# A fused attention and MLP block on one core: the second lower half of a step moved and written in place, and the keys' requests gathered

## The chip, the cores and the metric

The kernel runs on one core of a Trainium2 chip. The metric is device time in microseconds (us) of one launch; three runs of the kernel before gave 1380.38, 1377.33 and 1381.35 us, so a median of 1380.38 us. Traces come from a separate, profiled execution.

## The reference

For `x` of 1 x 2048 x 640 the kernel computes a parallel block: `xn` is the layer norm of `x`, and the output is `x` plus attention of `xn` plus an MLP of the layer norm of `xn`.

```
q, k, v = split(xn @ wqkv)                  # 32 heads of 20
p = softmax(q k^T * 20**-0.5)               # 2048 x 2048 for each head
A = (p v) @ wo
B = gelu(layernorm(xn) @ w1 + b1) @ w2 + b2 # 640 -> 1536 -> 640
out = x + A + B
```

All inputs are float32, and the kernel keeps nearly that precision on a 16-bit path: most operands are carried as a pair of 16-bit halves, an upper and a lower one, and a product is three matmuls of halves.

## The kernel before, in words

**Three stretches.** First (up to about 225 us) layer norm, the projections to queries, keys and values, and the splitting of weights into halves. Queries and keys go to DRAM scratch (`qkscr`), values stay on chip (`vfull`). Then the attention loop (about 225 to 1319 us), with the MLP's matmuls and the first part of the output projection poured between the attention's. Then the rest of the output projection.

**The attention loop.** Heads are taken four at a time (a quad). `VISITS` lists ten visits: quads 0 to 5 with four chunks of 512 queries each, then quads 6 and 7 twice with two chunks each: 32 rounds of one quad and one chunk (number 0 to 31 below). A round goes over 16 key blocks of 128 keys, two blocks to a step, so 256 steps. For each block `scores` (L766) makes two pairs of score tiles (L772, TensorE, into a PSUM pool of three) and ScalarE writes their exponentials to a float32 tile `pt` of 128 x 4 x 512 (L774).

**Split blocks.** In nine blocks of sixteen (`SPLIT`: 0, 2, 4, 6, 8, 9, 10, 12, 14) the probabilities are multiplied in halves. The upper half is no copy: `upper(pt)` (L776) reads the upper 16 bits of each float32 as bfloat16. The lower half is made by VectorE in `rest` (L780 to L786): `low = pt - upper(pt)`, written as float16 to a tile of its own from a rotation of two (L785). `pv` (L788) then multiplies with the values (L800): sixteen matmuls of 128 x 512 for the upper halves of two split blocks, four for each lower half, eight for a block that is not split. Block 9 is the only odd block that is split, so one step in eight has two lower halves; its step is the fifth of a round.

**Order around the change.** The instructions are recorded by hand in a fixed order (`manual_schedule`), and each engine works off its own list in that order. For an even block the list is: the block's scores and exponentials, `tick()`, `rest` of the previous step's odd block if that is split (block 9 alone), then `other()`, a measured portion of MLP or projection matmuls. For an odd block: scores and exponentials, `tick()`, `rest` of the even block of this step, then `pv` of the previous step. `tick()` advances every generator in the list `sides` by one piece. These pieces are VectorE's other work (the gelu chain L922 to L937, sums of the MLP's results L953, splitting of `wo` L739 to L744, the softmax division L883 to L911) and DMA requests on SyncE's queue, which issues them one after another. So VectorE's list around block 9 reads: lower half of block 8, the pieces of the tick of block 10, lower half of block 9, the pieces of the tick of block 11, lower half of block 10. TensorE's list there reads: scores of block 10, MLP matmuls, scores of block 11, `pv` of blocks 8 and 9, scores of block 12.

**Keys.** A visit needs its keys as two tiles of 61 rows twice (three copies of 20 rows, and a bias row, for each of two row groups). `load_keys` (L168) requests one half as six transfers from `qkscr` (L176) and two bias rows (L180), spread over five ticks, the bias rows last. The first half for the next visit is asked for at block 8 of a visit's last round, the second half at the first step of the visit, in `sides` behind the queries of the next round (`load_queries`, L148), which come one transfer a tick. Block 8 of that first round is the first to read the second half.

Of the kernel before, what the change touches and what calls it, by code (L numbers as in the profile page):

```python
# [10 lines left out]
F16 = mybir.dt.float16  # L11
# [7 lines left out]
P = 128  # L19
S, D, H, DH, F = 2048, 640, 32, 20, 1536  # L20
# [6 lines left out]
SPLIT = (1, 0) * 4 + (1, 1) + (1, 0) * 3  # L27
# [6 lines left out]
GRP = 2  # L34
# [14 lines left out]
def mha_mlp_kernel(tc, x, wqkv, wo, w1, b1, w2, b2, out):  # L49
    nc = tc.nc  # L50
# [3 lines left out]
    with (  # L54
# [17 lines left out]
        bscr = dram.tile([H + 1, S], F16, name="bscr")  # L72
# [75 lines left out]
        def load_queries(v, cc):  # L148

            q = VISITS[v][0]  # L150
            qs = stp.tile([P, 2, 512], F16, tag="qs", name="qs")
            qss[v, cc] = qs
            cols = slice(cc * 512, (cc + 1) * 512)
            for a in range(2):
                for i in range(3):
                    nc.sync.dma_start(qs[64 * a + i * DH : 64 * a + (i + 1) * DH], rows_of(qkscr[(0, 0, 1)[i]], 0, q, a, cols))
                    yield
            for a in range(2):
                h = 4 * q + a
                nc.sync.dma_start(qs[64 * a + 60 : 64 * a + 61], bscr[h : h + 3 : 2, cols].rearrange("(o p) t -> o p t", o=1))  # L160
                yield

        def rows_of(scr, r0, q, a, cols):

            r = r0 + 4 * q * DH
            return (scr[r : r + 4 * DH, cols].rearrange("(p a d) t -> a d p t", p=2, a=2)[a])

        def load_keys(v, half):  # L168

            q = VISITS[v][0]  # L170
            ks = stp.tile([P, 2, S // 2], F16, tag="ks", name="ks")
            kss[v, half] = ks
            cols = slice(half * 1024, (half + 1) * 1024)
            for a in range(2):
                for i in range(3):
                    nc.sync.dma_start(ks[64 * a + i * DH : 64 * a + (i + 1) * DH], rows_of(qkscr[(0, 1, 0)[i]], D, q, a, cols))  # L176
                    if i != 1:
                        yield
            for a in range(2):
                nc.sync.dma_start(ks[64 * a + 60 : 64 * a + 61], bscr[H : H + 1, None, cols].to_broadcast([1, 2, S // 2]))  # L180
            yield

        def load_first():
            parts = load_queries(0, 0), load_keys(0, 0)
            for _ in range(8):
                for p in parts:
                    next(p, None)
                yield
            yield from load_keys(0, 1)
# [8 lines left out]
        with tc.tile_pool(name="pa", bufs=2) as pa, tc.tile_pool(name="pa1", bufs=1) as pa1, tc.manual_schedule():  # L198
# [378 lines left out]
            pt = [pts[0][:, 0], pts[0][:, 1], pts[1][:, 0], pts[1][:, 1]]  # L577
# [114 lines left out]
        with ExitStack() as scope:  # L692
# [3 lines left out]
            ptp = pool(name="pt", bufs=2 * GRP)  # L696
# [4 lines left out]
            sides, patient = [], []  # L701
# [11 lines left out]
            def tick():  # L713
                t, taken[0] = taken[0], 0.0
                for its in (sides, patient):
                    for it in list(its):
                        if its is patient and t > 0 and it not in free:
                            continue
                        free.discard(it)
                        r = next(it, self_end)  # L720
                        if r is self_end:
                            its.remove(it)
                        elif r == WAIT:
                            free.add(it)
                        else:
                            t += r or 0.0
# [39 lines left out]
            def scores(v, cc, kb, pair, pt):  # L766

                qs, ks = qss[v, cc], kss[v, kb // 8]
                ps = psS.tile([P, 2, 512], F32, tag="s", name="s")
                for a in range(2):  # L770
                    rows = slice(64 * a, 64 * a + 61)
                    nc.tensor.matmul(ps[:, a, :], ks[rows, pair, kb % 8 * P : (kb % 8 + 1) * P], qs[rows, pair, :],  # L772
                                     start=True, stop=True)
                nc.scalar.activation(pt[:, 2 * pair : 2 * pair + 2], ps, AF.Exp, scale=QS)  # L774

            def upper(pt):  # L776

                return pt.bitcast(BF16).rearrange("p a (n t) -> p a n t", t=2)[:, :, :, 1]

            def rest(unit):  # L780

                kb, pt = unit[2:]
                if SPLIT[kb]:
                    low = ptp.tile([P, 4, 512], F16, tag="low", name="low", bufs=2)
                    nc.vector.tensor_sub(low, pt, upper(pt))  # L785
                    unit.append(low)  # L786

# [338 lines left out]
            def chain():  # L1126
                yield from mlp()
                yield from projection()


            with tc.manual_schedule():
                fill = chain()
                credit = 0.0 - next(fill)
                rate = 1.265
                groups = [(v, cc, kb) for v, (_, ccs) in enumerate(VISITS) for cc in ccs for kb in range(0, NKB, GRP)]
                prev = None

                runs = []

                def other():  # L1140

                    nonlocal credit
                    if not runs:
                        unit = next(fill)
                        if unit is None:
                            credit = 0.0
                            return
                        n, cost = unit
                        k = max(round((cost - credit) / rate) + 1, math.ceil(cost / CHUNK))
                        runs.extend(n * (i + 1) // k - n * i // k for i in range(k))  # L1150
                    for _ in range(runs.pop(0)):
                        credit -= next(fill)

                for v, cc, kb0 in groups:
                    units = []
                    for kb in range(kb0, kb0 + GRP):
                        pt = ptp.tile([P, 4, 512], F32, tag="p", name="p")
                        units.append([v, cc, kb, pt])
                        for pair in range(2):
                            scores(v, cc, kb, pair, pt)  # L1160
                        reading[0] = kb % GRP > 0 and prev is not None and prev[-1][2] == NKB - 1
                        tick()
                        if kb % GRP == 0:
                            if prev and SPLIT[prev[1][2]]:
                                rest(prev[1])
                            credit += rate
                            other()
                        else:
                            if SPLIT[kb - 1]:
                                rest(units[0])  # L1170
                            if prev:
                                pv(prev)
                            else:

                                credit += rate
                                other()
                    prev = units
                    ccs = VISITS[v][1]
                    if kb0 == 0:
                        if cc != ccs[-1]:  # L1180
                            sides.append(load_queries(v, cc + 1))
                        elif v + 1 < len(VISITS):
                            sides.append(load_queries(v + 1, VISITS[v + 1][1][0]))
                        if v and cc == ccs[0]:
                            sides.append(load_keys(v, 1))
                    if kb0 == NKB // 2 and cc == ccs[-1] and v + 1 < len(VISITS):
                        sides.append(load_keys(v + 1, 0))
                if SPLIT[prev[1][2]]:
                    rest(prev[1])
                n = 0  # L1190
                reading[0] = False
                ended[0] = True

                def more(k):
                    nonlocal n
                    for _ in range(k):
                        n += 1
                        cost = next(fill, 0)
                        if isinstance(cost, tuple):
                            cost = next(fill)  # L1200
                        tick()
                        if cost == 0:
                            return False
                    return True

                more(2)
                pv(prev)
                while more(1):
                    pass
                while sides or patient:  # L1210
                    tick()
                flag = nc.values_load(badi, min_val=0, max_val=1)
# [91 lines left out]
```

## Time and profile before

| what | value |
|---|---|
| median of three runs | 1380.38 us |
| the profiled execution's own time | 1382.86 us |
| its span, first to last instruction | 1380.9 us |
| around the span | 2.0 us |
| ScalarE busy | 1121.6 us, 81% |
| VectorE busy | 1102.9 us, 80% |
| TensorE granted clock, mean of the span | 0.991 |

The time outside the span is start and end of the launch. A busy time is the sum over an engine's instructions; for TensorE, whose matmuls overlap, it is near the span whenever the array is fed at all. "Idle before" in a row is the time that the engine stood still ahead of that instruction, with the instruction that released it. In a timeline the columns are start, duration, engine, line, operation, output and input, count, and in brackets the idle time.

### The profile page before, as it was taken

The page shows a single profiled execution, that of the slowest core. Times are in us where ns is not written, and L with a number is a line of the kernel's source. Part 1 is how long each engine was busy: PE and PEld are TensorE (multiplying, and loading weights), DVE is VectorE, ACT ScalarE, POOL GpSimd, SP SyncE. Part 2 cuts the span into 40 slices and gives each one's busy share as a digit, 9 for nine tenths or more (in the row PEclk, how much of TensorE's full clock was granted, in tenths as well). Part 3 has the DMA queues.
Part 4 walks back from the last instruction along what each step waited for, and adds up shares of the span by engine and source line. Part 5 has one row for each costly group of instructions (what it writes and reads, how often), then busy time and mean ns, then how long its engine had stood idle before and what let it go on. Part 6 is the DMA issues. An engine that isn't in the chain of part 4 may idle for free.

```text
span 1380.9 us, 28562 instructions
## 1 busy us (share of the span) xinstructions
PE 1333.0 (97%) x11747; PEld 594.1 (43%) x11747; DVE 1102.9 (80%) x1224; ACT 1121.6 (81%) x1274; POOL 37.7 (3%) x86
## 2 busy tenths in 40 slices
PE   9999999999999999999999999999999999999998
PEld 6545545443434343433444334333333333333366
DVE  5766745998888898989888889888888888797842
ACT  6754425999999999999999999998988988898910
POOL 3000000000000000000000000000000000000000
PEclk8999999999999999999999999999999999999999
DMA  8868732010212132122202221222121212232266
GB/s 268 241 198 178 145 99 71 13 49 20 71 47 64 40 86 77 46 74 61 74 14 57 50 57 36 79 73 64 36 78 50 74 43 71 89 110 71 78 198 190
DMA packets 103477, 118.85 MB, mean 86 GB/s; under 512 B 23264, under 2 KB 73604, under 8 KB 103344
## 3 DMA queue, kind: packets, MB, share of 16 engines
q1 hardware_dynamic: 99872, 109.76, 28.0%
q0 software_dynamic: 2912, 6.90, 2.7%
q8 instruction: 93, 1.52, 0.5%
q14 instruction: 40, 0.33, 0.1%
q10 hardware_dynamic: 560, 0.34, 0.1%
HBM read 76.97 MB, written 37.19 MB: 83 GB/s over the span
## 4 chain that ended last, share of the span: by engine, by line
PE 69%; DVE 18%; DMA 5%; issue 4%; ACT 3%; SPq 1%; DVEq 0%; ACTq 0%; POOLq 0%
PE o L800 21%; PE s L772 14%; PE pu L986 9%; DVE low L785 9%; PE py L1016 9%; PE qkp L361 7%; PE z L1101 5%; PE vp L434 3%; ACT p L774 2%; DVE u L924 1%; DVE u L922 1%; DMA xnt<-row 1%; DVE hT L937 1%; DVE u L935 1%; DMA qkscr<-qkhl 1%
## 5 line engine op out<-in xcount | busy, mean ns | idle before, releaser
L774 ACT ACTIVATE p<-s 128x1024 f32<-128x1024 f32 x1024 | 976.0, 1038 | 81.7 <-PE s L772 69.2
L785 DVE TENSOR_TENSOR low<-p 128x2048 f16<-128x2048 f32 x288 | 654.7, 2282 | 73.9 <-ACT p L774 69.3
L800 PE MATMUL o<-p,vfull 128*32 128x512 bf16 (+1 forms) x4096 | 411.0, 481 | 0.0
L772 PE MATMUL s<-qs,ks 61*128 61x512 f16 x2048 | 314.0, 383 | 5.5 <-DMA oscr<-oa 2.4
L1016 PE MATMUL py<-w2t,hT 128*128 128x320 f16 x1152 | 181.0, 303 | 0.0
L986 PE MATMUL pu<-xm,w1t 128*128 128x256 f16 x1440 | 179.5, 275 | 0.0
L772 PEld LDWEIGHTS <-ks 61*128 61x128 f16 x2048 | 60.8, 94 | 268.0 <-issue 252.7
L986 PEld LDWEIGHTS <-w1t 128*128 128x128 f16 x1440 | 131.4, 98 | 65.0 <-issue 50.8
L800 PEld LDWEIGHTS <-vfull 128*32 128x32 f16 x3456 | 72.4, 95 | 192.7 <-issue 150.7
L1016 PEld LDWEIGHTS <-hT 128*128 128x128 f16 x1152 | 103.0, 98 | 88.9 <-issue 53.7
L800 PE MATMUL o<-low,vfull 128*32 128x512 f16 x1152 | 110.5, 379 | 31.7 <-DVE low L785 31.2
L361 PE MATMUL qkp<-xnt,wv 128*128 128x512 f16 x600 | 132.2, 382 | 0.0
L361 PEld LDWEIGHTS <-wv 128*128 128x128 f16 x600 | 58.9, 99 | 70.1 <-issue 1.7
L800 PEld LDWEIGHTS o<-p,vfull 128*32 128x32 f32 x1792 | 55.0, 108 | 45.4 <-issue 0.7
L434 PE MATMUL vp<-wv,xnt 128*128 128x320 f16 x480 | 66.9, 299 | 2.7 <-DVE qkhl L377 2.7
L1101 PE MATMUL z<-w1t,ot 128*128 128x320 f16 x480 | 67.4, 299 | 0.0
L376 ACT ACTIVATE qkhl<-qkp,qks 128x1024 f16<-128x1024 f32 (+1 forms) x24 | 23.2, 965 | 50.9 <-PE qkp L361 31.3
L922 DVE TENSOR_TENSOR u<-pu,r2f 128x512 f32<-128x512 f32 x48 | 33.1, 689 | 33.2 <-PE pu L986 32.1
L434 PEld LDWEIGHTS <-xnt 128*128 128x128 f16 x480 | 46.8, 98 | 21.3 <-issue 2.8
L1101 PEld LDWEIGHTS <-ot 128*128 128x128 f16 x480 | 46.0, 98 | 22.9 <-issue 5.5
L377 DVE SCALAR_TENSOR_TENSOR qkhl<-qkp,qks,qkhl 128x1024 f16<-128x1024 f32 (+1 forms) x24 | 26.5, 1104 | 31.7 <-ACT qkhl L376 31.7
L1058 DVE SCALAR_TENSOR_TENSOR acc<-z,sc,acc 128x320 f32<-128x320 f32 x32 | 17.6, 550 | 40.1 <-PE z L1101 40.0
(187 smaller groups left out, 657.0 us busy)
## 6 DMA issues: line engine op xcount, KB each, us to landing
qkscr<-qkhl SPq DMA_DIRECT2D x40, 256.0 KB
ks<-qkscr SPq DMA_DIRECT2D x120, 80.0 KB
qs<-qkscr SPq DMA_DIRECT2D x192, 40.0 KB
xt<-in_A_x_dram SPq DMA_DIRECT2D x16, 320.0 KB
xscr<-xnt SPq DMA_DIRECT2D x4, 1280.0 KB
xm<-xscr SPq DMA_DIRECT2D x8, 640.0 KB
xb<-in_A_x_dram SPq DMA_DIRECT2D x16, 320.0 KB
xb<-in_B_b_dram POOLq DMA_DIRECT2D x16, 320.0 KB, 4.3
```

What stands on the lines that cost most here:

```text
L361: nc.tensor.matmul(ps[:, i, :], wv[:, k, q, a, mm * P : (mm + 1) * P], xnts[c][:, k, b, :], start=(k + n == 0), stop=(k == KD - 1 and n == 2))
L376: nc.scalar.activation(hl[:, 0, i0:i1], ps[:, i0:i1], AF.Copy, scale=a)
L377: nc.vector.scalar_tensor_tensor(hl[:, 1, i0:i1], ps[:, i0:i1], a, hl[:, 0, i0:i1], ALU.mult, ALU.subtract)
L434: nc.tensor.matmul(ps[:, hf, :320], xnts[c][:, k, a, j * P : (j + 1) * P], wv[:, k, 2, b, hf * 320 : (hf + 1) * 320], start=(n == 0), stop ...
L772: nc.tensor.matmul(ps[:, a, :], ks[rows, pair, kb % 8 * P : (kb % 8 + 1) * P], qs[rows, pair, :], start=True, stop=True)
L774: nc.scalar.activation(pt[:, 2 * pair : 2 * pair + 2], ps, AF.Exp, scale=QS)
L785: nc.vector.tensor_sub(low, pt, upper(pt))
L800: nc.tensor.matmul(pv.o[32 * h : 32 * h + 32, :], src[:, at(h) : at(h) + 32], t[:, h], start=not pv.begun, stop=last, skip_group_check=True)
L922: nc.vector.tensor_mul(u, ps, r2f[:, None, :].to_broadcast([P, 2, MC]))
L986: nc.tensor.matmul(ps[:, i], w1v[:, k, (f + i) // 4, a, fo_ : fo_ + P], xnt[:, k, b, :], start=(n == 0), stop=(n == 3 * KD - 1))
L1016: nc.tensor.matmul(ps[:, :320], hTs[mc][:, f, a, j * P : (j + 1) * P], w2v[:, f, b, hf * 320 : (hf + 1) * 320], start=(n == 0), stop=(n == ...
L1101: nc.tensor.matmul(ps[:, :320], ot[:, k, a, j * P : (j + 1) * P], wov[:, k, b, h * 320 : (h + 1) * 320], start=(n == 0), stop=(n == 3 * KD ...
```

## The change

`rest` of block 9 is now recorded ahead of `tick()` of block 10, directly behind `rest` of block 8 on VectorE's list, and writes the float16 lower half into the lower 16 bits of each float32 of `pt` itself, with a stride of four bytes, in place of a tile from the rotation. The rotation of two then serves eight lower halves a round. `load_keys` requests the bias row of a row group first and all four transfers of a row group in one tick, so one half in two ticks, and the second half is put at the head of `sides`.

```diff
             for a in range(2):
+                nc.sync.dma_start(ks[64 * a + 60 : 64 * a + 61], bscr[H : H + 1, None, cols].to_broadcast([1, 2, S // 2]))
                 for i in range(3):
                     nc.sync.dma_start(ks[64 * a + i * DH : 64 * a + (i + 1) * DH], rows_of(qkscr[(0, 1, 0)[i]], D, q, a, cols))
-                    if i != 1:
-                        yield
-            for a in range(2):
-                nc.sync.dma_start(ks[64 * a + 60 : 64 * a + 61], bscr[H : H + 1, None, cols].to_broadcast([1, 2, S // 2]))
-            yield
+                yield
...
                 if SPLIT[kb]:
-                    low = ptp.tile([P, 4, 512], F16, tag="low", name="low", bufs=2)
+                    if kb % GRP:
+                        low = pt.bitcast(F16).rearrange("p a (n t) -> p a n t", t=2)[:, :, :, 0]
+                    else:
+                        low = ptp.tile([P, 4, 512], F16, tag="low", name="low", bufs=2)
                     nc.vector.tensor_sub(low, pt, upper(pt))
...
                         reading[0] = kb % GRP > 0 and prev is not None and prev[-1][2] == NKB - 1
+                        if kb % GRP == 0 and prev:
+                            rest(prev[1])
                         tick()
                         if kb % GRP == 0:
-                            if prev and SPLIT[prev[1][2]]:
-                                rest(prev[1])
                             credit += rate
                             other()
...
                         if v and cc == ccs[0]:
-                            sides.append(load_keys(v, 1))
+                            sides.insert(0, load_keys(v, 1))
...
-                if SPLIT[prev[1][2]]:
-                    rest(prev[1])
+                rest(prev[1])
```

The last hunk changes nothing that runs: `rest` itself asks `SPLIT`. TensorE's and ScalarE's instructions keep their order.

## The prediction

> **What bounds the kernel now.** I read the groups of instructions by line first (after the bar: busy us, mean ns of one, then the idle time of the engine before them and what ended it), then the timeline around the longest waits.
>
> ```profile
> L774 ACT ACTIVATE p<-s 128x1024 f32<-128x1024 f32 x1024 | 976.0, 1038 | 81.7 <-PE s L772 69.2 <-issue 2.7 <-ACT p L774 2.6
> L785 DVE TENSOR_TENSOR low<-p 128x2048 f16<-128x2048 f32 x288 | 654.7, 2282 | 73.9 <-ACT p L774 69.3 <-PE o L800 3.8
> L772 PE MATMUL s<-qs,ks 61*128 61x512 f16 x2048 | 314.0, 383 | 5.5 <-DMA oscr<-oa 2.4 <-DMA linv<-lt 1.2 <-DMA qs<-qkscr 1.0
> ...
> L800 PE MATMUL o<-low,vfull 128*32 128x512 f16 x1152 | 110.5, 379 | 31.7 <-DVE low L785 31.2
> ```
>
> ScalarE's largest wait is for scores, so TensorE sets the pace of the loop; and TensorE itself waits in the loop for two things: 31.2 us for lower halves (L800), and 5.5 us ahead of scores (L772), which read keys; there the releaser named is whichever transfer came last, and part 3 looks at what was late. I looked where the 31.2 us lie. This is VectorE, then TensorE, in round 0, blocks 8 to 12:
>
> ```profile
> 244.61 2.28 DVE L785 TENSOR_TENSOR low<-p 128x2048 f16<-128x2048 f32 x1
> 246.81 0.68 DVE L935 SCALAR_TENSOR_TENSOR u<-w,u 128x512 f32<-128x512 f32 x1
> 247.53 0.49 DVE L936 TENSOR_SCALAR hT<-u,sc 128x512 f16<-128x512 f32 x1
> 248.05 0.75 DVE L937 SCALAR_TENSOR_TENSOR hT<-u,sc,hT 128x512 f16<-128x512 f32 x1
> 248.72 4.49 DVE L785 TENSOR_TENSOR low<-p 128x2048 f16<-128x2048 f32 x2
> ```
> ```profile
> 247.50 1.09 PE L800 MATMUL o<-p,vfull 128*32 128x512 bf16 x16
> 248.41 0.40 PE L800 MATMUL o<-low,vfull 128*32 128x512 f16 x4
> 251.06 0.40 PE L800 MATMUL o<-low,vfull 128*32 128x512 f16 x4 [2.25 <-DVE low L785]
> ...
> 251.93 1.48 PE L986 MATMUL pu<-xm,w1t 128*128 128x256 f16 x12
> ...
> 254.34 0.39 PE L800 MATMUL o<-low,vfull 128*32 128x512 f16 x4
> 254.56 1.03 PE L800 MATMUL o<-p,vfull 128*32 128x512 f32 x8
> ```
>
> VectorE finishes block 8's lower half at 246.89, does three gelu instructions, and starts block 9's at 248.72; TensorE, which could have gone on at 248.41 + 0.22 (four such products take 254.56 - 254.34), stands until 251.06. In the 32 rounds, 13 have VectorE work between the two halves: L935 to L937 in seven, L928 in five, L739 in one. In the other 19 the halves already run back to back, and the move does nothing. Here is an L928 place, and the last of the 13:
>
> ```profile
> 1059.64 0.68 DVE L928 SCALAR_TENSOR_TENSOR w<-w,u 128x512 f32<-128x512 f32 x1
> 1060.25 4.49 DVE L785 TENSOR_TENSOR low<-p 128x2048 f16<-128x2048 f32 x2
> ```
> ```profile
> 1237.10 0.68 DVE L739 TENSOR_SCALAR wtmp<-w1t,s_o 128x320 f32<-128x320 f32 x2
> 1237.69 2.28 DVE L785 TENSOR_TENSOR low<-p 128x2048 f16<-128x2048 f32 x1
> ```
>
> **Part 1, the move.** Nothing is added to VectorE: the same 288 lower halves. At round 0 block 9's half starts 248.72 - 246.81 = 1.91 us earlier and ends at 249.09; TensorE goes on 0.05 later (the lag at 251.06: the half ends at 251.00), at 249.14. That is a gain of 1.91, with 0.5 of the wait left. But the gelu instructions now run behind it, so block 10's half starts when it did, at 248.72 + 2.21 = 250.93, and ends at 253.21. TensorE would now want it at 254.34 - 1.91 = 252.43 and waits until 253.26: 0.83 is given back, 1.08 kept. **VectorE's total is unchanged, so a gain lasts only as far as VectorE has slack behind it.** I carried each place forward one round like this, each engine in its order with the durations of the rows. "Kept" is what is left after that round (round 0 gives another 0.51 back early in round 1):
>
> | wait ends at | moved behind | gain | kept |
> |---|---|---|---|
> | 251.1, 285.7 | L935-937 | 1.91, 1.91 | 0.57, 0.57 |
> | 320.8 | L935-937 | 1.90 | 0.86 |
> | 818.0, 884.9 | L928 | 0.60, 0.60 | 0, 0 |
> | 955.8 | L935-937 | 1.91 | 1.91 |
> | 992.0 | L928 | 0.60 | 0.60 |
> | 1026.5 | L935-937 | 1.66 | 0 |
> | 1062.6 | L928 | 0.60 | 0.60 |
> | 1133.2 | L935-937 | 1.91 | 1.91 |
> | 1170.1 | L928 | 0.60 | 0.60 |
> | 1206.7 | L935-937 | 1.91 | 0.86 |
> | 1240.0 | L739 | 0.28 | 0 |
>
> Gained 16.4 us, kept **8.5 us**. At 1026.5 the gain goes because the next MLP group waits for L922 to read its PSUM bank. Each of ScalarE's tanh waits for L928, which comes 2.2 us later at five places; the carrying forward counts that. Bounds: all 16.4 kept, or none.
>
> **Part 2, in place.** A stride of four bytes on the output is not in the trace with this instruction. These rows have a float16 output cut into pieces of 20, and a packed one:
>
> ```profile
> L144 DVE TENSOR_TENSOR w2t<-wtmp,w2t 128x640 f16<-128x640 f32 x12 | 9.9, 825 | 0.4
> ...
> L446 DVE SCALAR_TENSOR_TENSOR vfull<-vp,vfull 128x640 f16<-128x640 f32 x9 | 7.4, 823 | 9.0 <-ACT vfull L444 9.0
> ```
>
> Equal, so I take the duration as unchanged (2.28); the far end, twice that, is a rival below. TensorE reads the strided half in 0.23 for four matmuls (its sixteen upper ones: 248.41 - 247.50, a quarter of it) where a packed one takes 254.56 - 254.34 = 0.22; 32 x 0.02 = **0.6 us** lost at most, and I take it. `pt` is held until the lower products, four matmuls longer than now, but the next exponentials to its buffer follow scores that stand behind those products on TensorE, so this is hidden. The upper products need no new wait: they read other bytes. The relieved rotation ends waits of VectorE alone, worth 0 here.
>
> **Part 3, the keys.** SyncE's queue ahead of the longest wait, and TensorE there:
>
> ```profile
> 1235.40 2.32 SPq L176 DMA_DIRECT2D ks<-qkscr  x6
> ...
> 1249.28 0.34 SPq L911 DMA_DIRECT2D oscr<-oa  x1
> 1249.67 1.17 SPq L180 DMA_DIRECT2D ks<-bscr  x2
> ```
> ```profile
> 1251.63 0.37 PE L772 MATMUL s<-qs,ks 61*128 61x512 f16 x1 [2.43 <-DMA oscr<-oa]
> ```
>
> The bias rows stand on SyncE's queue behind L911's transfer, which waits for VectorE until 1249.28. Asked for with the rows they go out by about 1239, 10 us ahead of the need at 1251.63 - 2.43 = 1249.2. The 1.2 and 1.0 us are block 8 of rounds 24 and 20: there the second half's last requests are two and three ticks later than the new ones. I count the row's whole 5.5 us, and 0.3 for the scores right behind, which run apart where they wait in pieces: **5.8 us**; the ends are 0 and that. Price: 2.32 + 1.17 = 3.5 us of issuing now stands in two ticks, ahead of the queries (due a round later) and of the division's loads (read four ticks later). I take nothing, with 2 us as the bound.
>
> **Part 4, the clock.** Stretches of 4 us behind long waits (columns: length, busy us of TensorE, its weight loads, VectorE, ScalarE and GpSimd with counts, granted clock, DMA share, GB/s):
>
> ```profile
> 252.00:256.00 4.00, 4.00 (x40) 1.71 (x40) 3.69 (x5) 3.75 (x5) 0.00 (x0) 1.00 0.02 4
> 956.00:960.00 4.00, 4.00 (x24) 1.85 (x20) 2.46 (x2) 1.94 (x2) 0.00 (x0) 0.57 0.00 0
> 1134.00:1138.00 4.00, 4.00 (x26) 1.53 (x28) 3.41 (x2) 2.89 (x4) 0.00 (x0) 0.57 0.00 0
> 1171.00:1175.00 4.00, 4.00 (x24) 1.51 (x26) 3.93 (x6) 3.00 (x4) 0.00 (x0) 0.57 0.00 0
> 1253.00:1257.00 4.00, 4.00 (x30) 1.49 (x31) 2.29 (x1) 3.03 (x4) 0.00 (x0) 0.57 0.20 37
> ```
> ```profile
> 955.76 0.40 PE L800 MATMUL o<-low,vfull 128*32 128x512 f16 x4 [2.80 <-DVE low L785]
> ...
> 956.67 2.74 PE L986 MATMUL pu<-xm,w1t 128*128 128x256 f16 x12
> ```
>
> After waits of 2.80 and 2.43 us the mean granted clock is 0.57 over 4 us, and the same behind the waits of the table that end at 1133.2 and 1170.1; behind the 2.25 us that end at 251.06 it stays 1.00. Twelve matmuls of one kind took 2.74 in place of 1.48. All four waits shrink (to 1.1, 0.6, 2.0 and 0), below every wait that cost clock. That is 1.3 us of TensorE each, 5 in all; carried forward beside part 1, where some of it meets VectorE's lower halves again, **2.9 us** stay. Ends: 0 and 5. The Trainium skill, "TensorE: Matmul & The Clock Gate", section "Why this matters for your kernels", warns of idle gaps over about 3 us; none here is that long, so by it these slow stretches aren't due to the waits, and the term would be 0. The trace has 0.57 behind gaps of 2.80 and 2.43, and I go by it.
>
> **Sum.** 8.5 + 5.8 + 2.9 - 0.6 = 16.6 us. Against the profiled execution, 1382.86 - 16.6 = 1366.3; that one is 2.5 above the median of the runs, 1380.38 - 16.6 = 1363.8. The tail behind the loop keeps its order and shifts as a whole. I predict **1364 us**.
>
> **Rivals.**
> - *VectorE gives it all back* (12%): the part 1 gain ends in waits for block 10's and 12's halves, as it does at 1026.5; of the clock only the keys' place (about 1) is saved. 5.8 + 1 - 0.6: 1374, or within 0.3% if a key wait also stays. For it: round 0 gives back 0.83 within one step. Against it: behind 955.8 nothing is given back.
> - *The keys still come late* (12%): the wait at block 8 only changes its releaser. 16.6 - 5.8: 1369 to 1370.
> - *Nothing is given back* (10%): 16.4 + 5.8 + 2.9 - 0.6 and more clock: 1353 to 1357. It needs VectorE ready at the next halves, against the 0.83 above.
> - *Half clock not from the waits* (6%): it returns at other places; 13.7 gained, 1366.7. Against it the four pairs above.
> - *The in-place write is dear* (6%), the slower side. Each of 32 halves takes x longer. At the 13 places TensorE waits x more; at the 19 others there is slack: from the rows below, the second half ends at 413.57 + 4.49 = 418.06, and its products were due at 418.54 + 0.22, so 0.65 with the lag. 13x + 19(x - 0.65) exceeds 16.6 + 4.1 from x = 1.03 on: halves of 3.3 us. At twice the duration, 60.6 - 16.6: 1424. Against it the equal rows of part 2.
>
> ```profile
> 413.57 4.49 DVE L785 TENSOR_TENSOR low<-p 128x2048 f16<-128x2048 f32 x2 [0.46 <-ACT p L774]
> ```
> ```profile
> 418.54 0.62 PE L800 MATMUL o<-low,vfull 128*32 128x512 f16 x8
> ```
>
> **How the numbers follow.** The forecast as it stands has 54%. Faster by over 0.3% (4.1 us, about what a measurement of this kernel can tell from no change): 54 + 12 + 10 + 6 + 5 of the first rival = 87%; within: 7%; slower: 6%. The range 1356 to 1374 takes in the first two rivals, the nearer part of the third and the ends of the clock; it leaves out the dear write and the corners.
>
> **What would show it.** After: "PE o <- DVE low" falls from 31.2 to about 20 us, its longest to about 2; some of it moves from block 9's to block 10's halves. "PE s <- DMA" is near zero. No stretch with a clock of 0.57 in the loop. The in-place halves take 2.28 us. Wrong if those are longer, or if waits for L922's bank or for block 10's halves take what block 9's lose.

## The result, and the profile after

| kernel | median us | runs | ratio to before | 95% interval |
|---|---|---|---|---|
| before | 1380.87 | 4 | | |
| changed | 1367.19 | 4 | 0.9903 | 0.9878 to 0.9927 |
| changed, timed again beside another 11 runs of before (1378.53) | 1365.37 | 6 | 0.9910 | 0.9894 to 0.9926 |

The change makes the kernel about 13 us faster. The forecast was 1364 us, 16.6 us faster; the range was 1356 to 1374. The total is near, but one of its four parts was wrong, and the loop (from the first to the last score of the attention loop) shows it.

Groups of instructions by line after (lines of the changed kernel: L769 for L772, L771 for L774; L785 and L800 keep their numbers):

```profile
L771 ACT ACTIVATE p<-s 128x1024 f32<-128x1024 f32 x1024 | 976.8, 1037 | 62.4 <-PE s L769 51.5 <-ACT p L771 2.6
L785 DVE TENSOR_TENSOR low<-p 128x2048 f16<-128x2048 f32 x256 | 583.5, 2281 | 58.3 <-ACT p L771 58.0
L769 PE MATMUL s<-qs,ks 61*128 61x512 f16 x2048 | 311.1, 382 | 0.0
...
L800 PE MATMUL o<-low,vfull 128*32 128x512 f16 x1024 | 100.6, 379 | 15.0 <-DVE low L785 14.8
...
L785 DVE TENSOR_TENSOR p<-p 128x2048 f16<-128x2048 f32 x32 | 84.0, 2625 | 0.1
...
L800 PE MATMUL o<-p,vfull 128*32 128x512 f16 x128 | 13.1, 393 | 14.3 <-DVE p L785 14.3
```

Three things are to be seen. Scores wait for keys no longer (0.0 where 5.5 us stood). The waits for lower halves, now in two rows because block 9's half lies in `p`, add up to 14.8 + 14.3 = 29.1 us: hardly less than the 31.2 before. And the 32 in-place halves take 2625 ns where the 256 packed ones take 2281.

The same place as in the prediction, round 0, VectorE and then TensorE:

```profile
240.56 2.28 DVE L785 TENSOR_TENSOR low<-p 128x2048 f16<-128x2048 f32 x1
242.76 2.63 DVE L785 TENSOR_TENSOR p<-p 128x2048 f16<-128x2048 f32 x1
245.29 0.68 DVE L935 SCALAR_TENSOR_TENSOR u<-w,u 128x512 f32<-128x512 f32 x1
246.00 0.49 DVE L936 TENSOR_SCALAR hT<-u,sc 128x512 f16<-128x512 f32 x1
246.52 0.75 DVE L937 SCALAR_TENSOR_TENSOR hT<-u,sc,hT 128x512 f16<-128x512 f32 x1
247.19 2.29 DVE L785 TENSOR_TENSOR low<-p 128x2048 f16<-128x2048 f32 x1
```
```profile
244.37 0.38 PE L800 MATMUL o<-low,vfull 128*32 128x512 f16 x4
245.45 0.41 PE L800 MATMUL o<-p,vfull 128*32 128x512 f16 x4 [0.70 <-DVE p L785]
...
249.53 0.40 PE L800 MATMUL o<-low,vfull 128*32 128x512 f16 x4 [0.62 <-DVE low L785]
```

The order is as forecast: block 9's half directly behind block 8's, the gelu chain behind both. The wait of 2.25 us is 0.70, and block 10's half has become late by 0.62.

The first and the last score of the attention loop, before, after, and in a second profile of the changed kernel:

```profile
L772 PE MATMUL s<-qs,ks x2048: 372/386/631, 224.8 to 1314.5; 61*128 61x512 f16 x187
```
```profile
L769 PE MATMUL s<-qs,ks x2048: 372/386/605, 220.8 to 1300.4; 61*128 61x512 f16 x187
```
```profile
L769 PE MATMUL s<-qs,ks x2048: 372/386/631, 217.2 to 1297.0; 61*128 61x512 f16 x187
```

The loop is 1089.7 us before and 1079.6 after: **10.1 us** of the 14.1 by which the two profiled spans differ. The other 4.0 us lie ahead of the first score. There the kernels differ only in how the first visit's keys are asked for (`load_first` calls `load_keys` too), and no price of that shows: the profiles with the old requests (before and three variants below) begin their loops at 218.7 to 224.8, and the changed kernel itself began its loop at 220.8 in one profile and at 217.2 in the other, and took 1079.6 and 1079.8 us for it. So below I compare loops too, worked out from such rows of one profiled execution each, beside the medians of whole runs.

### The profile page after: what moved, and what is told of

Read it like the earlier page. It is cut to its first block, busy times and chain, and to the rows that moved or that the text cites. A ratio compares the mean times of both kernels' runs of the same rounds, so it can differ in the third digit from the quotient of the medians.

```text
span 1366.8 us, 28513 instructions
## 1 busy us (share of the span) xinstructions
PE 1326.9 (97%) x11747; PEld 591.5 (43%) x11747; DVE 1110.7 (81%) x1224; ACT 1123.0 (82%) x1274; POOL 37.7 (3%) x86
## 4 chain that ended last, share of the span: by engine, by line
PE 62%; DVE 26%; DMA 5%; issue 4%; ACT 3%; SPq 1%; DVEq 0%; ACTq 0%
PE o L800 20%; PE s L769 13%; DVE low L785 10%; PE py L1016 9%; PE pu L986 8%; PE qkp L358 5%; PE z L1101 5%; DVE p L785 4%; PE vp L431 3%; DVE u L924 2%; DVE w L926 2%; DVE u L922 2%; DMA xnt<-row 1%; DMA qkscr<-qkhl 1%; ACT p L771 1%
## 5 line engine op out<-in xcount | busy, mean ns | idle before, releaser
L771 ACT ACTIVATE p<-s 128x1024 f32<-128x1024 f32 x1024 | 976.8, 1037 | 62.4 <-PE s L769 51.5
L785 DVE TENSOR_TENSOR low<-p 128x2048 f16<-128x2048 f32 x256 | 583.5, 2281 | 58.3 <-ACT p L771 58.0
L800 PE MATMUL o<-p,vfull 128*32 128x512 bf16 (+2 forms) x4224 | 423.6, 478 | 14.3 <-DVE p L785 14.3
L769 PE MATMUL s<-qs,ks 61*128 61x512 f16 x2048 | 311.1, 382 | 0.0
L769 PEld LDWEIGHTS <-ks 61*128 61x128 f16 x2048 | 60.2, 94 | 259.6 <-issue 255.6
L800 PEld LDWEIGHTS <-vfull 128*32 128x32 f16 x3456 | 73.8, 95 | 193.0 <-issue 150.5
L800 PE MATMUL o<-low,vfull 128*32 128x512 f16 x1024 | 100.6, 379 | 15.0 <-DVE low L785 14.8
L785 DVE TENSOR_TENSOR p<-p 128x2048 f16<-128x2048 f32 x32 | 84.0, 2625 | 0.1
L800 PEld LDWEIGHTS o<-p,vfull 128*32 128x32 f32 x1792 | 55.5, 108 | 43.0
L922 DVE TENSOR_TENSOR u<-pu,r2f 128x512 f32<-128x512 f32 x48 | 33.1, 690 | 29.8 <-PE pu L986 28.8
```

Source lines behind the costliest of these rows:

```text
L800: nc.tensor.matmul(pv.o[32 * h : 32 * h + 32, :], src[:, at(h) : at(h) + 32], t[:, h], start=not pv.begun, stop=last, skip_group_check=True)
L922: nc.vector.tensor_mul(u, ps, r2f[:, None, :].to_broadcast([P, 2, MC]))
```

## The experiments

Theory A, formed from the trace after: the move and the keys are worth what the prediction says, and the in-place write gives most of the move back, because it is 0.34 us longer. Rival B: VectorE's total sets the loop, so the move is worth little however the half is written.

### The parts one by one

The move alone, half still packed into a tile of the rotation:

```diff
+                        if kb % GRP == 0 and prev:
+                            rest(prev[1])
                         tick()
                         if kb % GRP == 0:
-                            if prev and SPLIT[prev[1][2]]:
-                                rest(prev[1])
```

> Only the second lower half's place in the order changes: ahead of the tick, but still written packed into a tile of the rotation; keys as before. Theory A (the trace after shows the in-place halves at 2.63 us where the packed ones take 2.28, and these 0.34 us times 32 eat what the move gains): packed, the move keeps the 8.5 us of the prediction's table and 2.9 us of clock, so 11.4 us faster, about 1369.5 us; block 9's halves take 2.28 us. Rival B (VectorE's total sets the loop, so the move gains nothing however the half is written): within 3 us of before.

The keys alone (both edits of `load_keys` and `sides.insert(0, ...)`):

> Only load_keys' grouping and its place in the list of pieces change. Both theories: the waits of scores for keys (5.5 us in the trace before) go, and one stretch of half clock behind the wait of 2.4 us at the last visit's start: 6 to 7 us faster, about 1374.5 us. If the keys were hidden anyway, no difference.

The in-place write alone:

```diff
-                    low = ptp.tile([P, 4, 512], F16, tag="low", name="low", bufs=2)
+                    if kb % GRP:
+                        low = pt.bitcast(F16).rearrange("p a (n t) -> p a n t", t=2)[:, :, :, 0]
+                    else:
+                        low = ptp.tile([P, 4, 512], F16, tag="low", name="low", bufs=2)
```

> Only the place that the second lower half is written to changes (into the upper tile's own low bits, stride of four bytes); it stays behind the tick, keys as before. Theory A: 32 halves at 2.63 us instead of 2.28; at the places where TensorE already waits for them each 0.34 us is paid in full, so 7 us slower, about 1388 us. Rival B: 0.34 us a round is hidden and the time is that of before.

The move and the keys, without the in-place write:

> The whole change without the in-place write: order and keys as changed, the second lower half packed into the rotation's tile. Theory A: 17 us faster than before (8.5 for the move, 5.8 for the keys, 2.9 of clock), about 1363.5 us, and so some 4 us (at least the 3 to 7 us that the in-place halves cost) faster than the changed kernel's 1367.2. Rival B: the same as the changed kernel, 1367.

The changed kernel once more, for the last row of the table:

> The changed kernel itself, timed beside before once more on the chip of the next runs. Theory A: about 9 us faster than before, 8 us slower than the kernel with the move and the keys but a packed lower half (whose loop was 8.4 us shorter in the traces).

The first four shared 17 runs of before, with a median of 1377.20 us; the changed kernel's row is from the runs beside 1378.53.

| kernel | median us | ratio, 95% interval | loop us | loop against before |
|---|---|---|---|---|
| move | 1367.28 | 0.9928, 0.9902 to 0.9954 | 1082.5 | -7.2 |
| keys | 1371.52 | 0.9954, 0.9938 to 0.9971 | 1085.4 | -4.3 |
| in place | 1390.17 | 1.0096, 1.0068 to 1.0125 | 1101.0 | +11.3 |
| move and keys | 1358.46 | 0.9874, 0.9845 to 0.9902 | 1071.2 | -18.5 |
| all three (the change) | 1365.37 | 0.9910, 0.9894 to 0.9926 | 1079.8 | -9.9 |

The in-place write alone makes the kernel slower, by more than the 7 us expected (its loop has seven stretches of half clock where before has four); with the other two parts it costs 1079.8 - 1071.2 = 8.6 us of loop. Rival B falls: the packed move gains. In the packed version round 0 reads, VectorE and TensorE:

```profile
238.52 4.49 DVE L782 TENSOR_TENSOR low<-p 128x2048 f16<-128x2048 f32 x2
242.93 0.68 DVE L932 SCALAR_TENSOR_TENSOR u<-w,u 128x512 f32<-128x512 f32 x1
```
```profile
243.06 0.40 PE L797 MATMUL o<-low,vfull 128*32 128x512 f16 x4 [0.35 <-DVE low L782]
247.18 0.40 PE L797 MATMUL o<-low,vfull 128*32 128x512 f16 x4 [0.66 <-DVE low L782]
```

The halves run back to back in 4.49 us, and TensorE waits 0.35 where the in-place one made it wait 0.70. Comparing the two loops round by round, by the starts of the scores, the in-place version loses 0.1 to 0.5 us in 23 of the 32 rounds, and 1.3 us in round 27, where a stretch of half clock is also counted; the rest of the rounds are alike.

The keys' waits in the kernel with the move alone:

```profile
L772 PE MATMUL s<-qs,ks 61*128 61x512 f16 x2048 | 312.8, 382 | 7.4 <-DMA ks<-bscr 2.8 <-DMA oscr<-oa 2.4 <-DMA ks<-qkscr 1.1
```

They rose from 5.5 to 7.4 us: a loop that runs ahead meets late keys earlier. That is 1.9 us of the 7.0 by which the two parts together (18.5 us of loop) gain more than apart (7.2 + 4.3). Another part is the clock: of stretches of half clock, counted in 3.41 us, the loop before has four, the one with the move two, the one with the keys five, and the one with both none.

### What makes the write dear

All 288 halves strided, but in a tile of their own, two of them interleaved in its words:

```diff
+            turns = [0]
+            wide = m1.tile([P, 4, 1024], F16, name="wide").rearrange("p a (n t) -> p a n t", t=2)
...
-                    low = ptp.tile([P, 4, 512], F16, tag="low", name="low", bufs=2)
+                    turns[0] += 1
+                    low = wide[:, :, :, turns[0] % 2]
```

> Move and keys as changed; all 288 lower halves are written with a stride of four bytes, but to a tile of their own (two halves interleaved in it), not in place. Theory A1 (the stride makes the write dear): all 288 take about 2.63 us, VectorE gets 98 us more to do, and the kernel is far slower than before, by 50 us or more. Theory A2 (writing into the tile that is being read makes it dear): all 288 take 2.28 us and the time is that of the packed version, 1358 to 1364.

Block 9's half in its own tile, but packed:

```diff
+                        low = pt.bitcast(F16).rearrange("p a t -> p (a t)")[:, : 4 * 512].rearrange("p (a n) -> p a n", a=4)
```

> Move and keys as changed; block 9's lower half goes into its own tile, but packed, into the first quarter... that is the first half of the bytes of each partition's float32 row, so the upper halves of its first two heads are overwritten before TensorE reads them (that part of the result is changed). A1 (stride): these 32 take 2.28 us. A2 (same tile): 2.63 us.

Strided apart, without another half in the same words (`low = wide[:, :, :, 0]`):

> Move and keys as changed; all 288 lower halves with a stride of four bytes in a tile of their own, always the same half of its words, so TensorE never reads beside a write (each write waits for the reads of the one before; only the duration of the write is of interest, not the time of the kernel). A3 (the stride alone costs): 2.46 us, as with two interleaved halves. A4 (what cost there was TensorE reading the same words' other half): 2.28 us.

All 288 in place with the stride:

> Move and keys as changed, and all 288 lower halves in place, with the stride. A5 (writing in place costs beyond the stride): all 288 take about 2.63 us, 98 us more for VectorE. A6 (block 9's 2.63 comes of its place in the order, beside TensorE's upper products): block 9's take 2.63, the other 256 about 2.46 as in a tile apart.

The rows of the halves in these four, in that order (ns: least, median, longest):

```profile
L785 DVE TENSOR_TENSOR wide<-p x288: 2352/2466/2515, 221.4 to 1450.2; 128x2048 f16<-128x2048 f32 x144
```
```profile
L785 DVE TENSOR_TENSOR p<-p x32: 2267/2284/2293, 245.2 to 1293.5; 128x2048 f16<-128x2048 f32 x32
```
```profile
L783 DVE TENSOR_TENSOR wide<-p x288: 2349/2446/2483, 223.1 to 1983.7; 128x2048 f16<-128x2048 f32 x144
```
```profile
L782 DVE TENSOR_TENSOR p<-p x288: 2456/2623/2774, 221.8 to 1333.6; 128x2048 f16<-128x2048 f32 x144
```

Neither A1 nor A2 held as stated. Packed into the tile that is being read: 2.28 us, so being in place costs nothing by itself. Strided into another tile: 2.45 to 2.47 us, with or without a neighbour in the same words (A4 falls). Strided and in place: 2.62 us wherever it stands in the order (block by block the medians are 2.61 to 2.63; A6 falls). So the stride costs 0.16 to 0.18 us for 2048 elements a partition, and as much again when the strided write goes into the tile that is being read. Why the second part comes is not settled: whether the read and the write meet in the same words or only in the same tile was not tried apart. The times of the two kernels with one shared tile (1517.71 and 2053.83 us, one run each) are no price of the stride: there a half and the products of the one before wait for one another, 127.9 and 513.1 us of TensorE waiting. Nor is that of the packed half in its own tile (1370.84 us): there the upper products, whose bytes it overwrites, wait for it. All halves in place cost 1401.27 us in its one run.

### Which half of the keys' edit counts

Only the place in the list:

```diff
-                            sides.append(load_keys(v, 1))
+                            sides.insert(0, load_keys(v, 1))
```

> Before, with the second half of the keys put at the head of the pieces, and nothing else: its eight transfers still take five ticks. If the grouping is what counts: TensorE's waits for keys stay near 5.5 us, time as before within 2 us. If the place in the list counts: the waits of rounds 20 and 24 (2.2 us) go.

Only the grouping, in the order before:

> Before, with the keys asked for in two ticks, bias rows first, but the second half still behind the queries in the list. If the grouping is what counts: no wait of scores for keys is left, and the loop is as short as with both, about 1085.4 us where before has 1089.7.

Scores waited 4.9 us with the head of the list alone (loop 1089.3, that is -0.4) and 0.0 with the grouping alone (loop 1081.8, -7.9). The whole runs, one of each, took 1376.93 and 1372.91 us beside 1378.20. The grouping, with the bias rows first, takes away all of these waits; for the place in the list these profiles show no gain. The grouped loop is 3.6 us shorter here than the one with both edits, but these are single profiles, and the one with both had five stretches of half clock in its loop, this one three.

### A version that goes further

Half packed, move and keys, and the first half of each step ahead of its tick too:

```diff
+                        if kb % GRP and SPLIT[kb - 1]:
+                            rest(units[0])
                         tick()
...
-                            if SPLIT[kb - 1]:
-                                rest(units[0])
```

> Move and keys as changed, second half packed, and also the first lower half of every step ahead of its tick. If TensorE's remaining waits for lower halves (23.4 us in the packed version) come from VectorE's other pieces standing ahead of them: up to 10 us faster than the packed version, 1350 to 1356. Rival (VectorE's total is the limit there, and what is put off holds the MLP's PSUM bank): waits of MLP matmuls for L922 and L953 take their place, and the time is 1358 to 1368.

1347.88 us, ratio 0.9782 (0.9766 to 0.9798), better than expected: the loop is 1060.8 us, 10.4 shorter than the packed version's (with the move and the keys). TensorE's rows in it, for the waits that were to go and for those that were to come:

```profile
L797 PE MATMUL o<-low,vfull 128*32 128x512 f16 x1152 | 109.9, 378 | 15.5 <-DVE low L782 15.3
```
```profile
L1013 PE MATMUL py<-w2t,hT 128*128 128x320 f16 x1152 | 178.5, 300 | 1.7 <-DVE u L919 1.5
```

The waits for halves are 15.3 us where the packed version has 23.4, and the MLP's wait for its PSUM bank stays at 1.5: VectorE's other pieces have room to come later. All waits of TensorE in the loop are 7.7 us shorter than in the packed version; the other 2.7 us are not traced to a cause.

## Why the prediction was right in its total, point by point

- **What bounds the loop, and where the waits lie: right.** Each edit moved the waits that the prediction named, and the loop followed.
- **Part 1, the move: right in mechanism and size.** In the packed versions the gains at the 13 places and what is given back behind them are the table's within about 0.1 us at nearly all of them (round 0: 1.91 gained and 0.84 given back, against 1.91 and 0.83). Rounds 21 and 26 kept more than the 1.91 forecast (2.3 and 2.4): their stretches of half clock are gone, which the prediction counts in part 4.
- **Part 2, in place: wrong, and the step that failed.** "So I take the duration as unchanged (2.28)": it was 2.63. The nearest row that I leant on, L446, writes pieces of 20 adjacent elements; it says nothing on single ones. A longer half was also the prediction's own sign of being wrong. TensorE's waits for halves and for L922's read of the MLP's PSUM bank are together 31.7 us before, 25.3 in the packed version with the keys and 31.1 in the changed kernel: of 6.4 us that the move saves when packed, the in-place write leaves 0.6. The rival "the in-place write is dear" was the right mechanism at a third of its deciding size; but its slack formula would give 13 x 0.34 = 4.4 us, and 8.4 to 8.6 us of loop were measured. One reason is in the trace before: the slack of 0.65 us was read from one round, and not all of the 19 have it. In round 25 nothing stands between the halves, and TensorE waits for block 9's all the same (VectorE, then TensorE):

```profile
1091.92 4.49 DVE L785 TENSOR_TENSOR low<-p 128x2048 f16<-128x2048 f32 x2
```
```profile
1096.46 0.40 PE L800 MATMUL o<-low,vfull 128*32 128x512 f16 x4 [0.84 <-DVE low L785]
```

  Rounds 4 and 6 wait too (0.16 and 1.02 us). Worked out product by product from the traces of the two moved versions, block 9's products wait 5.2 us longer in place than packed, 3.7 of it in the 13 rounds and 1.5 in the others; other waits add 0.6. The remaining 2.6 us of the 8.4 are no waits: one stretch of half clock is among them, and the rest is not traced to a cause. The 0.6 us for TensorE's strided reads fits the rows of round 0 after: four strided products take 0.41 us, the packed ones beside them 0.38 and 0.40, so 0.3 to 1.0 us over 32 rounds.
- **Part 3, the keys: right.** 5.5 us of waits went to 0.0. The loop gained 4.3 us with both edits and 7.9 with the grouping alone, where 5.8 and some clock were forecast. That a faster loop alone would have waited longer (7.4) was not foreseen. The price put on the earlier requests does not show.
- **Part 4, the clock: right in direction, its threshold wrong, its size partly chance.** Of four stretches of half clock three are gone. "Below every wait that cost clock" is refuted by the trace after, TensorE and then the stretch behind:

```profile
1160.70 0.41 PE L800 MATMUL o<-p,vfull 128*32 128x512 f16 x4 [2.12 <-DVE p L785]
...
1161.61 2.85 PE L1016 MATMUL py<-w2t,hT 128*128 128x320 f16 x10
```
```profile
1161.00:1165.00 4.00, 4.00 (x22) 1.60 (x18) 3.96 (x5) 2.46 (x3) 0.00 (x0) 0.57 0.00 0
```

  A wait of 2.12 us cost clock here, and one of 2.25 had not in round 0 before. With the keys grouped alone, nearly the same wait at the same place of round 0 did:

```profile
249.13 0.40 PE L797 MATMUL o<-low,vfull 128*32 128x512 f16 x4 [2.26 <-DVE low L782]
```

  So the length of the wait alone does not decide. The traces show what does. Within each execution, the stretches of half clock last 3.41 us or a multiple of it and start on one grid of 3.413 us (before: at 956.52, 1134.02, 1171.56 and 1253.48, which are 52, 11 and 24 steps apart). A wait can fall into one step of this grid or be divided between two. Here is round 0 in steps of the grid, before, and then with the keys grouped alone (the columns as in the prediction):

```profile
246.55:249.96 3.41, 2.26 (x29) 0.85 (x27) 3.34 (x5) 3.13 (x4) 0.00 (x0) 1.00 0.00 0
249.96:253.37 3.41, 2.31 (x22) 1.33 (x23) 3.25 (x2) 1.54 (x2) 0.00 (x0) 1.00 0.00 0
```
```profile
247.28:250.69 3.41, 1.56 (x15) 0.84 (x15) 3.41 (x2) 1.27 (x2) 0.00 (x0) 1.00 0.00 0
250.69:254.10 3.41, 3.41 (x24) 1.31 (x25) 2.46 (x4) 2.50 (x4) 0.00 (x0) 0.50 0.03 5
```

  Before, the 2.25 us are divided: TensorE is idle for 1.15 us of one step and 1.10 of the next, and the clock stays. With the keys grouped, 1.85 us fall into one step, and the next step has half clock. The same holds for every step in the loops of twelve profiles (all but the two kernels with one shared tile): each stretch of half clock begins behind a step with 1.64 to 2.93 us idle, and no step with up to 1.63 us idle is followed by the start of one; from 1.64 to 1.78 us there are steps of both kinds, above 1.78 all are followed by half clock. Shorter waits than 2.12 us cost clock too when they lie in one step: the 1.93 us of round 1 did with both edits of the keys and did not before. The waits that the prediction left at 1.1, 0.6 and 2.0 us are 0.88, 0.43 and 1.80 in the packed version with the keys, which has no stretch of half clock in its loop, and 1.21, 0.77 and 2.12 in the changed kernel: there the longer half put the last one high enough. Where the grid falls differs from one execution to the next, so of the forecast 2.9 us a part is chance.
- **The total.** 16.6 us were forecast for work in the loop; 10.1 came there: 6.1 us of shorter waits (0.6 and 5.5), and 4.0 in which TensorE works for less time. Three stretches of half clock fewer would be about 3.9 of these, an estimate at the prediction's 1.3 us each. Between the profiled runs 4.0 more lie ahead of the loop, where two profiles of the same kernel also differ by 3.6; the medians differ by 13.2 to 13.7, with an interval from about 10 to 17 us, and how much of that lies in the loop they can't tell. That the total fell inside the range although part 2 is off by about 8 us is luck of the range's width: it was not drawn for a dear write, but 1380.4 - 10.1 = 1370.3 lies in it too. The measurement of whole runs alone would not have shown the error.

The Trainium skill, "Vector Engine (DVE) Microarchitecture Reference", section "Measured stream behaviour on trn2", says that a port keeps its full rate only while its elements come as runs of two adjacent 4-byte words or more, and lists a write that hops by 4 KiB at every 4-byte element with 1.71 ns an element in place of 1.05. That rule speaks against the in-place write and I had not weighed it. The runs agree in direction; for 2-byte elements at a 4-byte stride the size is smaller here, (2446 - 2284) / 2048 = 0.08 ns an element into another tile and 0.17 in place.

## What to carry to other kernels

Where one engine's output is needed at a fixed point of another's order, look at what stands ahead of it in that engine's list: putting the needed work first gained 7.2 us of loop here alone, and 18.5 together with the earlier keys, with no instruction less, as long as what is put off has slack, and the gain must be followed to the next thing needed from the same engine. A transfer whose last piece comes late is all late: group its pieces. Before an output is given a new access pattern, find a row with that same pattern, not one that is merely not contiguous; a part of a change that costs can hide in a total that comes out right.

## What the runs showed of the hardware

- VectorE's float32 subtraction with a float16 output, 128 x 2048: 2.28 us packed (in the tile being read or in another), 2.45 us with a stride of four bytes in another tile, 2.62 us with that stride in the tile being read.
- The stretch ahead of the loop varies between executions with the same code: the first score stood at 220.8 and 217.2 us in two profiles of the changed kernel.
- TensorE's clock fell to half for 3.41 us at a time, on a grid of 3.413 us. In twelve profiles it fell behind grid steps with 1.64 us of idle TensorE or more, always above 1.78 and never below 1.64; a wait of 2.25 us that was divided between two steps cost nothing, one of 1.93 in one step did.
